# A second expert block on whole columns, its attention jobs inside the first block, and weight tiles scaled one step ahead

## The chip, the cores and the metric

The kernel runs on one core of a Trainium2 chip. The metric is the device time of one execution in microseconds (us); the time quoted for a version is the median of its timed runs. The profile is of one further execution.

## The reference

Three stages follow one another. First a recurrent attention (WKV) over 768 positions, for 4 batch entries and 8 heads of width 48; then two mixture layers over the 3072 tokens, the first of width 2048, the second, behind an RMS norm, gated and of width 1536. All inputs and the output are float32.

```python
def _attn_ref(r, k, v, w, u):
    for t in range(S):
        cur = np.einsum('bhd,bhe->bhde', u[None] * kt, vt)
        y[:, :, t] = np.einsum('bhd,bhde->bhe', rt, state + cur)
        state = wt[:, :, :, None] * state + np.einsum('bhd,bhe->bhde', kt, vt)

def _moe_ref(x, w_in, w_out):
    h = x @ w_in
    return (h * np.clip(h + 3.0, 0.0, 6.0) / 6.0) @ w_out

def _moe2_ref(x, w_gate, w_val, w_out, rms_g):
    xn = x / np.sqrt(np.mean(x * x, axis=-1, keepdims=True) + 1e-06) * rms_g
    g = xn @ w_gate
    return (g / (1.0 + np.exp(-g)) * (xn @ w_val)) @ w_out
```

## The kernel before, in words

The sequence is cut into 6 chunks of 128 positions. A chunk `c` of one batch entry `b` is a **job** (24 of them, job number 4c + b). The four jobs of a chunk give 512 token columns, and the first mixture layer takes these 512 columns as one **block**. Six blocks of the first layer come one after another, and behind them six of the second layer.

A block of the first layer is 16 tiles `f` of its width. Each is a **step**: `ff1` multiplies the tile's first weights with the 512 columns (all three parts of 128 rows), ScalarE and VectorE apply the activation (`emit_act`), and `ff2` multiplies the result with the tile's second weights into three accumulators. `ff2` of a step is put off by two steps (`todo`, L615), so that the activation has time. `LAGS` (L33) says for each block how many of its first tiles are done in two halves of 256 columns: first all of them on the left half, then all on the right half, then the remaining tiles on 512 columns. With `LAGS` (5, 8, 0, ...) block 0 has steps 0 to 20 (ten half steps, eleven whole ones), block 1 has steps 21 to 44 (sixteen half steps, eight whole ones), and block 2 begins at step 45.

Block 0 multiplies float32 weights directly (`emit_h_f32`, `emit_out_f32`). All other blocks use weights and activations that are split in two float32r parts and make three passes (`PASS`); the first part is a rounded copy, the second the rest.

The weights of the first layer arrive as 64-bit words. For each tile, `Weight.load` fetches the words into `raw` (L132), `scale` makes a scaled copy `mag` on ScalarE (L140), `bits` puts the float32 words together in three VectorE operations (L145 to L148) and has SyncE's queue copy them to their place `wpair` (L153), and `parts` splits them for the blocks behind block 0 (L159 on ScalarE, L160 on VectorE). `raw` has two buffers and `mag` one.

The order of all engines is that in which the program is written (`pin` fixes it). Lists named `before`, `between` and `behind` hold what is written ahead of a step's `ff1`, between its `ff1` and the put-off `ff2`, and behind that. `plan(j, n)` (L442) spreads job `j` over the steps from `n` on: the two scans of the decay (`scans`, L182) and GpSimd's `bonus1` (L209, L210) at step n; `muls` (L205), the reduction `bonus2` (L214) and GpSimd's `decay` at n+1; `fill` (eight ScalarE copies, L240), TensorE's `pe_a` (L259) and `pe_kt` (L247), and VectorE's masked copy `choose` (L265) at n+2; `pe_y` (L295, L301) and `pe_u` (L274) at n+3, with `copy_y` (L307) and eight small transfers `x<-y` (L310 to L313); and `split` (L323 on ScalarE, L324 on GpSimd), which writes the job's 128 columns of `xt`, the input of the block, at n+5. `pe_y` reads what `choose` wrote. The loads of job j+2 are written behind step n+3, the load of `rks` for job j+1 behind step n+1.

Jobs 0 to 3 are done in the prologue and in steps 0 to 6. Jobs 4 to 7, which feed block 1, start at steps 11, 15, 19 and 23 (L470), so jobs 6 and 7 end inside block 1: the right half of block 1 begins at step 29. Jobs of later chunks start at `first[c] - 18 + 4 * b`, that is 27, 31, 35 and 39 for the four that feed block 2. `begun` (L476) says at which step a weight tile is scaled and put together: `scale` is written ahead of that step's `ff1`, `bits` behind it, and then the load of the tile two further on. `parts` of tile f stands ahead of step f + 11. The norm of block 0's output (`Norm`) takes its operations at steps 24 to 36.

```python
    for f, n in begun.items():
        before[n] += [wa[f].scale]
        behind[n] += [wa[f].bits]
        if f + 2 < F1:
            behind[n] += [wa[f + 2].load]
    for f in range(F1):
        before[f + 11] += [wa[f].parts]
```

Of the kernel before, what the change touches and what calls it, by code (L numbers as in the profile page):

```python
# [9 lines left out]
F32 = mybir.dt.float32  # L10
F32R = mybir.dt.float32r
U32 = mybir.dt.uint32
U64 = mybir.dt.uint64
# [4 lines left out]
B, H, S, D = 4, 8, 768, 48  # L18
# [4 lines left out]
DM = H * D  # L23
KT = DM // 128
F1 = 2048 // 128
# [4 lines left out]
NB = 3 * F2 // 2  # L30
NX = 5
NE = 10
LAGS = (5, 8, 0, 0, 0, 0)  # L33


@with_exitstack
def kernel(
# [17 lines left out]
    def pool(stack, name, bufs=1, **kw):  # L55
        return stack.enter_context(tc.tile_pool(name=name, bufs=bufs, **kw))
# [9 lines left out]
    wp = pool(ctx, "wp", side="left")  # L66
    xt_p = pool(ctx, "xt", 2, side="left")
    rg_p = pool(ctx, "rg", 3, side="left")
    nm_p = pool(ctx, "nm", side="left")
    actx = ctx.enter_context(ExitStack())  # L70
    at_p = pool(actx, "at", 2, side="left")
    a1_p = pool(actx, "a1", side="left")
# [1 line left out]
    st_p = pool(tctx, "st", 2, side="left")  # L74
# [32 lines left out]
    def pin():  # L107
        fresh = []
        for x in reversed(nc.cur_bb.bb.instructions):
            if x.name in pinned:  # L110
                break
            fresh.append(x)
        for x in reversed(fresh):
            pinned.add(x.name)
            if x.engine in ENGINES:
                if x.engine in newest:
                    tc.add_manual_dep(x, newest[x.engine], NOSYNC, reason="program order")
                newest[x.engine] = x.name
# [2 lines left out]

    mag_bufs = 1

    class Weight:
        def __init__(self, src, dst, pairs):
            self.src, self.dst, self.pairs, self.near = src, dst, pairs, False

        def load(self):  # L130
            self.raw = st_p.tile([128, 2 * DM], U64, tag="raw", name="raw", bufs=2)
            nc.sync.dma_start(out=self.raw, in_=self.src.rearrange("p a n -> p (a n)"))  # L132

        def words(self):
# [1 line left out]
            return bits[:, :, 0], bits[:, :, 1]  # L136

        def scale(self):
            self.mag = st_p.tile([128, 2 * DM], F32, tag="mag", name="mag", bufs=mag_bufs)
            nc.scalar.activation(out=self.mag, in_=self.words()[1].bitcast(F32), func=AF.Copy, scale=2.0 ** -112)  # L140

        def bits(self):
# [230 lines left out]
    def emit_out(acc, slot, g, first, last, cols, parts=False):  # L373
        for m in range(KT):
            for j, (l, r) in enumerate(PASS):
                nc.tensor.matmul(  # L376
                    acc[m][:, cols], slot[:, l, m * 128:(m + 1) * 128], g[:, r, :],
                    start=(first and j == 0), stop=(parts or last and j == 2),
                    skip_group_check=parts and not (first and j == 0))
# [50 lines left out]
    jobs = [Job(c, b) for c in range(NC_) for b in range(B)]  # L430
    wa = [Weight(wa_d[f], None, False) for f in range(F1)]
    whole, halves = slice(0, TOK), (slice(0, HT), slice(HT, TOK))
    steps, first = [], []
    for c, lag in enumerate(LAGS):
        first.append(len(steps))
# [4 lines left out]
    before, between, behind = ([[] for _ in steps] for _ in range(3))  # L440

    def plan(j, n):  # L442

        jb = jobs[j]
        before[n] += [jb.scans, jb.bonus1]
        before[n + 1] += [jb.muls, jb.bonus2, jb.decay]
        before[n + 2] += [jb.fill]
        between[n + 2] += [jb.pe_a, jb.pe_kt, jb.choose, jb.copy_kt]
        between[n + 3] += [jb.pe_y, jb.pe_u, jb.copy_y, jb.add_u]
        if j + 2 < len(jobs):  # L450
            behind[n + 3] += [lambda: jobs[j + 2].load("w", "rk", "v")]
        if j + 1 < len(jobs):
            behind[n + 1] += [lambda: jobs[j + 1].load("rks")]
        before[n + 5] += [jb.split]


    j0, j1, j2, j3 = jobs[:B]
# [8 lines left out]
    for j, n in enumerate((1, 2, 3, 4)):  # L466
        behind[n] += [jobs[j].decay]
        between[n + 1] += [jobs[j].pe_kt, jobs[j].copy_kt]
        between[n + 2] += [jobs[j].pe_u, jobs[j].add_u]
    for j, n in zip(range(B, 2 * B), (11, 15, 19, 23)):  # L470
        plan(j, n)
    for c in range(2, NC_):
        for b in range(B):
# [1 line left out]

    begun = {f: f - 2 for f in range(2, W1)} | {7: 7, 8: 8} | {f: f + 1 for f in range(9, F1)}  # L476
    for f, n in begun.items():
        before[n] += [wa[f].scale]
        behind[n] += [wa[f].bits]
        if f + 2 < F1:  # L480
            behind[n] += [wa[f + 2].load]
    for f in range(F1):
        before[f + 11] += [wa[f].parts]
    behind[7] += [lambda: jobs[4].load("w", "rk", "rks", "v")]
    behind[9] += [lambda: jobs[5].load("w", "rk", "v")]

    def norm_plan(c, n, last):

# [10 lines left out]
    def ff1(c, f, cols):  # L499
        n = cols.stop - cols.start  # L500
        ps = ps_h.tile([128, n], F32, tag="h", name="hps")
        if c == 0:
            if cols.start:
                wa[f].x = wpair[f][:, :, 1, :].bitcast(F32)
            emit_h_f32(wa[f].x[:, 0], xts[c][:, :, :, cols], ps)
            g = rg_p.tile([128, n], F32, tag="g", name="g")
            emit_act(ps, n, g)
        else:
            emit_h(wpair[f][:, 0], xts[c][:, :, :, cols], ps)
            a = rg_p.tile([128, n], F32, tag="a", name="a", bufs=2)  # L510
            emit_act(ps, n, a)
            g = emit_split(a, n)
        x = wa[f].x[:, 1] if c == 0 else wpair[f][:, 1]
        todo.append(lambda: ff2(c, f, cols, g, x))

    def ff2(c, f, cols, g, x):
# [6 lines left out]
        else:  # L523
            emit_out(acc, x, g, first, last, cols, LAGS[c] > 0)
        if last:
            norms[c] = Norm(c, acc)

    def run(fs):
        for x in fs:
            x()  # L530

    def load_x(c):
        x = xt_p.tile([128, KT, 2, TOK], F32R, tag="xt", name="xt")
        raw = b_p.tile([128, KT, TOK], F32, tag="xraw", name="xraw", bufs=1)
        nc.sync.dma_start(out=raw, in_=xn_d[c])
        xns[c] = x

        def part(k):
            nc.scalar.activation(out=x[:, k, 0, :], in_=raw[:, k, :], func=AF.Copy)
            nc.vector.tensor_tensor(  # L540
                out=x[:, k, 1, :], in0=raw[:, k, :], in1=x[:, k, 0, :].bitcast(F32), op=ALU.subtract)
        return part
# [22 lines left out]
    nc.sync.dma_start(out=ub, in_=u_d.to_broadcast([128, DM]))  # L565
    nc.sync.dma_start(out=gain, in_=g_d)
    wa[2].load()
    wa[3].load()
    nc.vector.memset(dd, 0.0)
    nc.vector.memset(half, 0.5)  # L570
    nc.vector.memset(eps, 1e-6)
# [4 lines left out]
        wa[f].dst = wpair[f]  # L576
        wa[f].near = f < 2
    run((j0.scans, j0.pairs, j0.pe_bonus, j0.muls, j0.fill, j0.pe_a, j1.scans, j1.pairs, j1.pe_bonus, j1.muls))
    run((j0.choose, j1.fill, j1.pe_a, j0.pe_y0, wa[0].scale, wa[0].bits, j1.choose, j1.pe_y0))
    run((j0.copy_y0, wa[1].scale, wa[1].bits, j1.copy_y0, j2.scans))  # L580
    pin()


    for n, (c, f, cols) in enumerate(steps):
        if n == W1:
            sctx.close()
            wp2 = pool(ctx, "wp2", side="right", reuse_waits="tile")
            wpair += [wp2.tile([128, 2, 2, DM], F32R, name=f"wpair{i}") for i in range(W1, F1)]
            for i in range(W1, F1):
                wa[i].dst = wpair[i]  # L590
        if n == first[1]:
            tctx.close()
        if n == first[NC_ - 1]:
            actx.close()
            st_p = pool(ctx, "st2", 2, side="left", reuse_waits="tile")
            mag_bufs = 2
            b_p = pool(ctx, "bp", 2, side="left", reuse_waits="tile")
            bw_p = pool(ctx, "bw", side="left", reuse_waits="tile")
            begun2 = {f: f * NE // F1 for f in range(F1) if (f + 1) * NE // F1 > f * NE // F1}
            extra += [bw_p.tile([128, 2, 2, DM], F32R, name=f"bpair{i}") for i in range(NX)]  # L600
            wb = [Weight(wb_d[i], extra[i] if i < NX else wpair[i - NX], True) for i in range(NB)]
            wb[0].load()
            wb[1].load()
        run(before[n])
        if c == NC_ - 1:
            if f == 4:
                part = load_x(0)
            if 8 <= f < 8 + KT:
                part(f - 8)

            if f - 2 in begun2:
                wb[begun2[f - 2]].parts()
        ff1(c, f, cols)
        run(between[n])
        while len(todo) > 2:  # L615
            todo.pop(0)()
        if c == NC_ - 1 and f in begun2:
            wb[begun2[f]].scale()
        run(behind[n])
        if c == NC_ - 1 and f in begun2:  # L620
            wb[begun2[f]].bits()
            wb[begun2[f] + 2].load()
        pin()
# [145 lines left out]
```

## Time and profile before

| | |
|---|---|
| median of 3 runs | 1025.42 us (1025.32 to 1026.27) |
| the profiled execution: its own time | 1027.49 us |
| its span, first to last instruction | 1025.7 us |
| TensorE (PE) busy | 982.3 us, 96% of the span |
| TensorE weight load (PEld) | 782.4 us, 76% |
| VectorE (DVE) | 484.3 us, 47% |
| ScalarE (ACT) | 393.9 us, 38% |
| GpSimd (POOL) | 346.4 us, 34% |
| mean granted TensorE clock | 0.987 |

The busy share of an engine is a mean over stages that differ much, so the slices and the stretches by stage are read before it. PEclk is the granted clock as a share of full speed: 1.00 is 2.4 GHz, and a lower value is a mean of stretches at 2.4 and at 1.2 GHz. Matmuls are pipelined, so the time from one start to the next start says what one costs; the duration of a row is longer than that. A matmul of float32 operands shows as two records.

### The profile page before, as it was taken

To read this page: it belongs to the slowest core of one execution; us is meant where nothing else is said; L and a number is where in the kernel's file an instruction comes from. 1 tells how busy PE (TensorE), PEld (TensorE's weight loads), DVE (VectorE), ACT (ScalarE), POOL (GpSimd) and SP (SyncE) were. 2 spreads that over 40 slices of the span, in tenths; PEclk is the share of its full clock that TensorE was granted. 3 is DMA by queue.
4 is the path that set the end of the run, shared out by engine and by line. 5 is a ranking of instruction groups with operands and counts; after the bars stand their busy time and mean duration, and the time that the engine had idled before them with its cause. 6 is when DMAs were issued, how large, how long until landed. Compare 5 with 4: busy or idle time off the path is not lost.

```text
span 1025.7 us, 13752 instructions
## 1 busy us (share of the span) xinstructions
PE 982.3 (96%) x5385; PEld 782.4 (76%) x5385; DVE 484.3 (47%) x627; ACT 393.9 (38%) x753; POOL 346.4 (34%) x306
## 2 busy tenths in 40 slices
PE   5797998889999999999999999999999999999998
PEld 4674457877888888787787788888888888888886
DVE  7848756665457646665389996112112112112111
ACT  3433535544544454455356554222222222222212
POOL 0002214545465574565353352222222222222221
PEclk9899989999999999999999999999999999999999
DMA  8557522333322332231242450200100100100000
GB/s 320 173 202 276 183 90 81 123 130 102 122 76 79 120 134 75 109 92 64 100 144 103 156 182 1 93 1 1 62 1 1 61 1 1 62 1 1 31 1 31
DMA packets 36768, 91.92 MB, mean 90 GB/s; under 512 B 5984, under 2 KB 17120, under 8 KB 36704
## 3 DMA queue, kind: packets, MB, share of 16 engines
q1 hardware_dynamic: 36704, 91.05, 25.6%
q8 instruction: 42, 0.69, 0.3%
q14 instruction: 22, 0.18, 0.0%
HBM read 71.37 MB, written 9.44 MB: 79 GB/s over the span
## 4 chain that ended last, share of the span: by engine, by line
PE 79%; DVE 9%; ACT 4%; DMA 4%; issue 3%; SPq 1%; POOL 0%; ACTq 0%; DVEq 0%; POOLq 0%
PE o L376 27%; PE gps L347 14%; PE vps L347 14%; PE hps L347 12%; DMA raw<-in_dram 3%; PE aps L259 2%; PE yps L301 2%; DVE x L146 2%; PE o L359 2%; PE yps L295 1%; DVE x L148 1%; PE hps L353 1%; DVE a L365 1%; PE ktp L247 1%; DVE w L182 1%
## 5 line engine op out<-in xcount | busy, mean ns | idle before, releaser
L376 PE MATMUL o<-g,wpair 128*128 128x512 f32 (+1 forms) x1287 | 306.1, 382 | 0.0
L376 PEld LDWEIGHTS o<-g,wpair 128*128 128x128 f32 x1287 | 230.4, 189 | 48.8 <-issue 0.7
L370 POOL TENSOR_TENSOR g<-s,g 128x512 fp32r<-128x512 f32 x72 | 96.8, 1344 | 338.4 <-ACT g L369 338.4
L663 DVE TENSOR_TENSOR s<-s,vps 128x512 f32<-128x512 f32 x72 | 49.5, 687 | 301.3 <-PE vps L347 300.4
L347 PE MATMUL hps<-xt,wpair 128*128 128x512 f32 (+1 forms) x792 | 182.9, 375 | 3.4 <-POOL xt L324 2.1
L370 POOL TENSOR_TENSOR g<-a,g 128x512 fp32r<-128x512 f32 (+1 forms) x88 | 113.9, 1295 | 196.7 <-ACT g L369 185.4
L347 PEld LDWEIGHTS hps<-xt,wpair 128*128 128x128 f32 x792 | 139.7, 188 | 34.2 <-POOL xt L324 2.3
L347 PE MATMUL vps<-xt,wpair 128*128 128x512 f32 x486 | 120.4, 392 | 0.0
L365 DVE SCALAR_TENSOR_TENSOR a<-a,hps 128x512 f32<-128x512 f32 (+1 forms) x88 | 55.7, 633 | 129.3 <-ACT a L364 129.2
L347 PE MATMUL gps<-xt,wpair 128*128 128x512 f32 x432 | 107.2, 392 | 0.0
L369 ACT ACTIVATE g<-s 128x512 fp32r<-128x512 f32 x72 | 45.5, 632 | 159.7 <-DVE s L663 159.7
L347 PEld LDWEIGHTS vps<-xt,wpair 128*128 128x128 f32 x486 | 91.2, 188 | 20.5
L660 ACT ACTIVATE s<-gps 128x512 f32<-128x512 f32 x72 | 43.0, 597 | 158.7 <-PE gps L347 158.7
L347 PEld LDWEIGHTS gps<-xt,wpair 128*128 128x128 f32 x432 | 81.0, 188 | 18.3
L364 ACT ACTIVATE a<-hps,half 128x512 f32<-128x512 f32 (+1 forms) x88 | 56.6, 643 | 96.1 <-PE hps L347 89.5
L369 ACT ACTIVATE g<-a 128x512 fp32r<-128x512 f32 (+1 forms) x88 | 52.2, 593 | 87.8 <-DVE a L365 86.2
L182 DVE TENSOR_TENSOR_SCAN w<-w,dd 128x520 f32<-128x520 f32 x48 | 74.8, 1559 | 4.6 <-DMA w<-in_dram 2.9
L240 ACT ACTIVATE a<-iperm,cb 128x128 f32<-128x128 f32 x192 | 58.5, 387 | 0.1
L347 PE MATMUL gps<-xt,bpair 128*128 128x512 f32 x216 | 53.0, 390 | 0.0
L209 POOL TENSOR_TENSOR rks<-rks 128x384 f32<-128x384 f32 x20 | 29.2, 1460 | 64.7 <-DMA rks<-in_dram 64.7
L347 PEld LDWEIGHTS gps<-xt,bpair 128*128 128x128 f32 x216 | 40.5, 188 | 8.8
L140 ACT ACTIVATE mag<-raw 128x768 f32<-128x768 f32 x34 | 30.6, 901 | 41.1 <-DMA raw<-in_dram 30.3
(85 smaller groups left out, 1055.8 us busy)
## 6 DMA issues: line engine op xcount, KB each, us to landing
raw<-in_dram SPq DMA_DIRECT2D x34, 768.0 KB, 4.7
w<-in_dram SPq DMA_DIRECT2D x24, 520.0 KB, 3.8
rk<-in_dram SPq DMA_DIRECT2D x24, 512.0 KB, 4.6
rks<-in_dram SPq DMA_DIRECT2D x20, 384.0 KB, 4.7
v<-in_dram SPq DMA_DIRECT2D x24, 256.0 KB, 4.8
wpair<-x SPq DMA_DIRECT2D x16, 384.0 KB, 3.2
xn<-x SPq DMA_DIRECT2D x6, 768.0 KB, 4.0
xraw<-xn SPq DMA_DIRECT2D x6, 768.0 KB, 5.0
```

Of the source, the lines that this page charges most:

```text
L140: nc.scalar.activation(out=self.mag, in_=self.words()[1].bitcast(F32), func=AF.Copy, scale=2.0 ** -112)
L182: nc.vector.tensor_tensor_scan(out=x, data0=x, data1=dd.rearrange("p a h j -> p (a h j)"), initial=0.0, op0=ALU.mult, op1=ALU.add)
L209: nc.gpsimd.tensor_tensor(out=x, in0=x, in1=self.rks[:, 1, :], op=ALU.mult)
L240: nc.scalar.activation(out=self.head(h), in_=iperm, func=AF.Copy, scale=self.cb[:, h, :])
L347: nc.tensor.matmul(ps, slot[:, l, k * 128:(k + 1) * 128], xt[:, k, r, :], start=(k == 0 and j == 0), stop=(k == KT - 1 and j == 2))
L364: nc.scalar.activation(out=a, in_=ps, func=AF.Relu, scale=1.0 / 6.0, bias=half)
L365: nc.vector.scalar_tensor_tensor(out=a, in0=a, scalar=1.0, in1=ps, op0=ALU.min, op1=ALU.mult)
L369: nc.scalar.activation(out=g[:, 0, :], in_=a, func=AF.Copy)
L370: nc.gpsimd.tensor_tensor(out=g[:, 1, :], in0=a, in1=g[:, 0, :].bitcast(F32), op=ALU.subtract)
L376: nc.tensor.matmul(acc[m][:, cols], slot[:, l, m * 128:(m + 1) * 128], g[:, r, :], start=(first and j == 0), stop=(parts or last and j == ...
L660: nc.scalar.activation(out=s, in_=gp, func=AF.Silu)
L663: nc.vector.tensor_tensor(out=s, in0=s, in1=vp, op=ALU.mult)
```

## The change

Block 1 is done on whole columns (`LAGS` (5, 0, ...)): it has 16 whole steps, 21 to 36, and block 2 begins at step 37. Jobs 4 to 7 start at steps 6, 9, 12 and 15, three steps apart, and end at step 20, inside block 0. The first loads of jobs 4 and 5 stand behind steps 2 and 4. `parts` of tile f stands ahead of step f + 17, so 12 of 16 tiles are split inside block 1. The buffers of `raw` are three and of `mag` two; `scale` stands at the end of the step ahead of that of `bits`, and the load is for the tile three further on. The pool of the norm's tiles is opened on the other side of the memory when block 1 begins.

```diff
-LAGS = (5, 8, 0, 0, 0, 0)
+LAGS = (5, 0, 0, 0, 0, 0)
...
-            self.raw = st_p.tile([128, 2 * DM], U64, tag="raw", name="raw", bufs=2)
+            self.raw = st_p.tile([128, 2 * DM], U64, tag="raw", name="raw", bufs=2 if self.pairs else 3)
...
-            self.mag = st_p.tile([128, 2 * DM], F32, tag="mag", name="mag", bufs=mag_bufs)
+            self.mag = st_p.tile([128, 2 * DM], F32, tag="mag", name="mag", bufs=2)
...
-    for j, n in zip(range(B, 2 * B), (11, 15, 19, 23)):
+    for j, n in zip(range(B, 2 * B), (6, 9, 12, 15)):
         plan(j, n)
...
-        before[n] += [wa[f].scale]
+        (behind[n - 1] if n else before[n]).append(wa[f].scale)
         behind[n] += [wa[f].bits]
-        if f + 2 < F1:
-            behind[n] += [wa[f + 2].load]
+        if f + 3 < F1:
+            behind[n] += [wa[f + 3].load]
     for f in range(F1):
-        before[f + 11] += [wa[f].parts]
-    behind[7] += [lambda: jobs[4].load("w", "rk", "rks", "v")]
-    behind[9] += [lambda: jobs[5].load("w", "rk", "v")]
+        before[f + 17] += [wa[f].parts]
+    behind[2] += [lambda: jobs[4].load("w", "rk", "rks", "v")]
+    behind[4] += [lambda: jobs[5].load("w", "rk", "v")]
...
-    wa[3].load()
...
-    run((j0.choose, j1.fill, j1.pe_a, j0.pe_y0, wa[0].scale, wa[0].bits, j1.choose, j1.pe_y0))
-    run((j0.copy_y0, wa[1].scale, wa[1].bits, j1.copy_y0, j2.scans))
+    run((j0.choose, j1.fill, j1.pe_a, j0.pe_y0, wa[0].scale, wa[0].bits, wa[3].load, j1.choose, j1.pe_y0))
+    run((j0.copy_y0, wa[1].scale, wa[1].bits, wa[4].load, j1.copy_y0, j2.scans))
...
         if n == first[1]:
             tctx.close()
+            nm_p = pool(ctx, "nm", side="right", reuse_waits="tile")
```

Three places show how the order moves. The changed file has three or four lines fewer at its head, so L140 of before is L137 of the change.

On ScalarE, at the job whose `fill` comes first behind a weight tile. Before, steps 12 and 13, with job 4's `fill`:

```order
L140 ACTIVATE mag<-raw 128x768
L159 ACTIVATE wpair_116<-wpair_116 128x2x384
L364 ACTIVATE g<-hps,half 128x512
L240 ACTIVATE a<-iperm,cb 128x128 x8
L140 ACTIVATE mag<-raw 128x768
L159 ACTIVATE wpair_117<-wpair_117 128x2x384
L364 ACTIVATE g<-hps,half 128x512
L252 ACTIVATE kt<-ktp 128x512
```

The change, end of step 10 and step 11, with job 5's `fill` and, ahead of it, the `split` of job 4:

```order
L137 ACTIVATE mag<-raw 128x768
L320 ACTIVATE xt<-x 128x3x128
L237 ACTIVATE a<-iperm,cb 128x128 x8
L361 ACTIVATE g<-hps,half 128x512
L249 ACTIVATE kt<-ktp 128x512
L137 ACTIVATE mag<-raw 128x768
```

The scaled copy and the split weights no longer stand between `fill` and the activation `g<-hps`; the `split` of the job before now stands ahead of `fill`.

On VectorE, from a job's `muls` to its `choose`. Before, job 5, steps 16 and 17:

```order
L205 TENSOR_TENSOR rk<-rk,w 128x8x64 x2
L214 TENSOR_REDUCE cb<-rks 128x8
L160 TENSOR_TENSOR wpair_120<-wpair_120 128x2x384
L365 SCALAR_TENSOR_TENSOR g<-g,hps 128x512
L145 TENSOR_SCALAR x<-raw 128x768
L146 SCALAR_TENSOR_TENSOR x<-raw,x 128x768
L148 SCALAR_TENSOR_TENSOR x<-mag,x 128x768
L160 TENSOR_TENSOR wpair_121<-wpair_121 128x2x384
L365 SCALAR_TENSOR_TENSOR g<-g,hps 128x512
L265 COPY_PREDICATED a<-mask,aps 128x512 x2
```

The change, job 6, steps 13 and 14:

```order
L202 TENSOR_TENSOR rk<-rk,w 128x8x64 x2
L211 TENSOR_REDUCE cb<-rks 128x8
L362 SCALAR_TENSOR_TENSOR g<-g,hps 128x512
L142 TENSOR_SCALAR x<-raw 128x768
L143 SCALAR_TENSOR_TENSOR x<-raw,x 128x768
L145 SCALAR_TENSOR_TENSOR x<-mag,x 128x768
L362 SCALAR_TENSOR_TENSOR g<-g,hps 128x512
L262 COPY_PREDICATED a<-mask,aps 128x512 x2
```

The two weight splits between `muls` and `choose` are gone from block 0.

On TensorE, from the first `ff1` of block 1 on. Before, steps 21 to 23, with job 6 (`st_108`):

```order
L347 MATMUL hps<-xt,wpair_115 128x256 x9
L259 MATMUL aps<-rk 128x128 x8
L247 MATMUL ktp<-ident,rk 128x128 x4
L359 MATMUL o_432<-g,wpair_598 128x512
...
L347 MATMUL hps<-xt,wpair_116 128x256 x9
L295 MATMUL yps<-rk,st_108 64x128 x8
L301 MATMUL yps<-a,v 64x128 x8
L274 MATMUL ups<-v,kt 64x48 x8
```

The change, with job 8 (`st_103`):

```order
L344 MATMUL hps<-xt,wpair_112 128x512 x9
L256 MATMUL aps<-rk 128x128 x8
L244 MATMUL ktp<-ident,rk 128x128 x4
L356 MATMUL o_431<-g,wpair_619 128x512
...
L344 MATMUL hps<-xt,wpair_113 128x512 x9
L292 MATMUL yps<-rk,st_103 64x128 x8
L298 MATMUL yps<-a,v 64x128 x8
L271 MATMUL ups<-v,kt 64x48 x8
```

The matmuls between a job's `pe_a` and its `pe_y` have 512 columns in place of 256, and the job at that place feeds block 2, not block 1.

## Rows read from the trace of the kernel before

**Rows 1.** The page, busy tenths of TensorE in 40 slices of 25.6 us.

```profile
PE   5797998889999999999999999999999999999998
```

**Rows 2.** Stretches: length, then busy us per engine, granted clock, DMA share, GB/s.

```profile
61.10:147.40 86.30, 77.77 (x333) 43.37 (x332) 58.65 (x79) 32.97 (x62) 16.01 (x17) 0.94 0.55 195
147.40:258.10 110.70, 98.65 (x838) 84.61 (x837) 65.10 (x98) 54.84 (x124) 56.13 (x62) 0.95 0.32 107
258.10:341.00 82.90, 82.90 (x564) 66.73 (x563) 49.38 (x64) 39.54 (x84) 47.60 (x42) 1.00 0.28 94
```

**Rows 3.** TensorE's waits from 24 to 259 us: total us, times, longest.

```profile
PE yps L295 <- DVE a L265: 8.5, 3, 3.4
PE yps L295 <- POOL g L370: 6.7, 2, 4.4
PE ktp L247 <- ACT st L281: 3.0, 3, 1.4
...
PE hps L347 <- POOL xt L324: 2.1, 1, 2.1
```

**Rows 4.** Timeline of TensorE behind job 4's `pe_y`: start us, us, operation.

```profile
102.87 3.95 PE L359 MATMUL o<-g,wpair 128*128 128x512 f32 x6
```

**Rows 5.** ScalarE's longest kind of wait from 61.1 to 147.4 us: total us, times, longest.

```profile
ACT mag L140 <- DMA raw<-in_dram: 27.5, 6, 8.3
```

**Rows 6.** Timeline of TensorE across the end of block 0.

```profile
140.10 2.74 PE L359 MATMUL o<-g,wpair 128*128 128x512 f32 x6
142.67 2.74 PE L353 MATMUL hps<-xt,wpair 128*128 128x512 f32 x6
...
148.98 1.16 PE L259 MATMUL aps<-rk 48*128 48x128 f32 x16
...
150.56 2.74 PE L359 MATMUL o<-g,wpair 128*128 128x512 f32 x6
...
154.30 0.67 PE L295 MATMUL yps<-rk,st 64*64 64x128 f32 x16
...
156.37 1.98 PE L359 MATMUL o<-g,wpair 128*128 128x512 f32 x4
```

**Rows 7.** Groups by form: count, busy us, mean ns, idle before.

```profile
L182 DVE TENSOR_TENSOR_SCAN w<-w,dd 128x520 f32<-128x520 f32 x48 | 74.8, 1559 | 4.6 <-DMA w<-in_dram 2.9
...
L205 DVE TENSOR_TENSOR rk<-rk,w 128x512 f32<-128x512 f32 x48 | 43.6, 947 | 0.1
...
L160 DVE TENSOR_TENSOR wpair<-wpair 128x768 fp32r<-128x768 f32 x16 | 15.8, 989 | 18.3 <-ACT wpair L159 18.3
...
L159 ACT ACTIVATE wpair<-wpair 128x768 fp32r<-128x768 f32 x16 | 13.3, 831 | 0.0
...
L364 ACT ACTIVATE g<-hps,half 128x512 f32<-128x512 f32 x11 | 7.4, 677 | 9.1 <-PE hps L353 9.1
```

**Rows 8.** Timeline of ScalarE in steps 3 and 4; in brackets the idle time before, and what ended it.

```profile
48.05 0.90 ACT L140 ACTIVATE mag<-raw 128x768 f32<-128x768 f32 x1 [3.06 <-DVE x L148]
...
53.45 0.89 ACT L140 ACTIVATE mag<-raw 128x768 f32<-128x768 f32 x1 [1.83 <-DMA raw<-in_dram]
```

**Rows 9.** Timeline of ScalarE at job 4: `fill`, `copy_y`, `split`.

```profile
91.29 2.43 ACT L240 ACTIVATE a<-iperm,cb 128x128 f32<-128x128 f32 x8
...
104.76 0.59 ACT L307 ACTIVATE y<-yps 128x512 f32<-128x512 f32 x1
...
111.81 0.52 ACT L323 ACTIVATE xt<-x 128x384 fp32r<-128x384 f32 x1 [0.70 <-DMA x<-y]
```

**Rows 10.** Timelines of VectorE and GpSimd during job 4's scans.

```profile
79.66 1.89 DVE L182 TENSOR_TENSOR_SCAN w<-w,dd 128x520 f32<-128x520 f32 x1
...
80.54 1.81 POOL L210 TENSOR_TENSOR rks<-rks,ub 128x384 f32<-128x384 f32 x1
```

**Rows 11.** Timelines of VectorE and TensorE at job 13, in block 2.

```profile
282.94 1.37 DVE L265 COPY_PREDICATED a<-mask,aps 128x512 f32<-128x512 uint32 x2
...
286.48 0.67 PE L295 MATMUL yps<-rk,st 64*64 64x128 f32 x16
```

More of the change, by code (lines that the diff above doesn't have):

```diff
@@ L68 @@
     rg_p = pool(ctx, "rg", 3, side="left")
-    nm_p = pool(ctx, "nm", side="left")
     actx = ctx.enter_context(ExitStack())
@@ L118, in pin @@
                 newest[x.engine] = x.name
-    mag_bufs = 1
     class Weight:
@@ L595 @@
             st_p = pool(ctx, "st2", 2, side="left", reuse_waits="tile")
-            mag_bufs = 2
             b_p = pool(ctx, "bp", 2, side="left", reuse_waits="tile")
```

## The prediction

> **What bounds the kernel now.** I read the slices first, then the stretches by stage, then the waits of TensorE, and last what stands ahead of the late instruction on its own engine. In the slices [rows 1] TensorE is busy nine tenths or more from the tenth slice to the last but one; the lower digits lie in the first quarter, and that is where this change works. The stretches [rows 2] put it in time: from the first matmul of step 6 (61.1 us) to that of step 21 (147.4) TensorE is busy 77.8 of 86.3 us at a granted clock of 0.94, in block 1 (to 258.1) 98.6 of 110.7 at 0.95, while block 2, which has the same 16 tiles and four jobs, takes 82.9 us, is busy all of it and stays at 1.00. The two first stretches thus lose 8.5 and 12.1 us to idle time, and more to the clock's lower level.
>
> TensorE's own waits [rows 3] name `pe_y` first: 8.5 us for `choose`, and 6.7 us put down to GpSimd, and then the inputs `xt` of block 1's right half. After such a wait the clock is low: six records that take 2.74 us at full speed [rows 6] take 3.95 behind job 4's `pe_y` [rows 4]. The masked copy is late because VectorE and ScalarE are late, and ScalarE is late because the scaled copy `mag` stands ahead of its other work and waits for its weight tile: 27.5 us in six waits, the longest 8.3 [rows 5]. In block 1's half steps the cause is another: between a job's `pe_a` and `pe_y` TensorE has only two passes of 256 columns, half of what block 2 has there, so that `fill` and `choose` can't keep up.
>
> **The change part by part.**
>
> *Block 0, step 6 to step 21.* TensorE's work, if nothing waits: a float32 pass of 512 columns costs 142.67 - 140.10 = 2.57 us, a half one is taken at half of it, 1.29; a job's `pe_a` and `pe_kt` cost 150.56 - 148.98 = 1.58 and its `pe_y` and `pe_u` 156.37 - 154.30 = 2.07, together 3.65 [rows 6]. In these steps stand 20 whole and 10 half passes (ff1 of steps 6 to 20, ff2 of steps 4 to 18) and now four jobs: 51.4 + 12.9 + 14.6 = 78.9 us, where 86.3 were [rows 2]: -7.4, though two more jobs are done in it.
>
> *Block 1.* It has become block 2's shape: 82.9 us [rows 2], of which 68.3 without the four jobs is 2.13 a pass. Two of its first ff2 passes are float32 ones, + 2 x (2.57 - 2.13) = 0.9. So 83.8 in place of 110.7: -26.9. Whole in place of half columns is in this number; it is a small part of it.
>
> Both together take 162.7 us for 197.0. The 34.3 us between them are 20.6 of idle time and 13.7 of busy time (176.4 - 162.7), nearly all of which is work at the lower clock. So this counts on both: no idle time, and a clock that therefore stays up.
>
> *Scaling a step ahead.* Ahead of step 6 three waits of `pe_kt` for ScalarE sum to 3.0 us [rows 3]. In two of them a scaled copy stood in front, waiting 3.06 us for VectorE to free the one `mag`, and 1.83 us for the tile [rows 8]; the second buffer of `mag`, the third of `raw` and the earlier load remove both. The third wait is the job's own chain. Bounds 0 and 3.0; I take 1.5, since a chain of that kind remains at all three places. In block 0 the same edit removes the 27.5 us [rows 5], which cover the -7.4 above and are not counted again.
>
> *VectorE as cover.* It is busy 58.7 us of the 86.3 [rows 2]. Block 0 gains two full jobs: two scans, two `muls` (1.56 and 0.95 each, means over the run [rows 7]), a masked copy of 1.37 [rows 11] and an allowance of 1.0 for two small operations, 7.4 each; it loses six splits of 0.99 [rows 7]. 58.7 + 14.8 - 5.9 = 67.6 under 78.9: still covered, with less to spare. The earlier loads of jobs 4 and 5 cost nothing on the same ground: transfers have a share of 0.55 in this stretch [rows 2].
>
> *New waits.* (a) `split` of job 4 now stands ahead of job 5's `fill` on ScalarE and waits for eight `x<-y` transfers. From `copy_y` to `split` 111.81 - 104.76 = 7.05 us passed [rows 9]; with `split` 0.52, `fill` 2.43 [rows 9], the activation 0.68 [rows 7] and as much again on VectorE, `choose` 1.37 [rows 11], it ends 12.7 us behind the first `pe_y`. Until then TensorE has job 4's `pe_u` (about 0.5), three half passes of 1.29, three whole ones of 2.57 and job 5's `pe_a` and `pe_kt` of 1.58 to do: 13.7. So 1.0 us is left. If it fails, `pe_y` of job 5 waits and the two activations behind it, not yet due, don't. Behind `copy_y` SyncE's queue also holds job 6's loads and the next tile, which have two steps. (b) The split weights now stand ahead of `choose` in block 1: 0.83 on ScalarE and 0.99 on VectorE [rows 7], against 286.48 - 284.31 = 2.2 us by which block 2's `choose` is early [rows 11]. Each of (a) and (b) is bounded by 0 and the old wait of 3.4 [rows 3]; both come out near the edge of their cover, so I take 1.0 for each.
>
> *The pool for the norm* moves to other memory; no engine gets an instruction for it, and its tiles are first written in step 22, long behind the old tenants: 0. From block 2 on nothing changes, and TensorE has no gap there to be filled.
>
> **Sum.** -7.4 - 26.9 - 1.5 + 2.0 = -33.8 us. The profiled execution took 1027.49 us, which makes 993.7; it stands 2.1 above the median of the runs, so the median should go from 1025.4 to **991.6**.
>
> **Rivals.**
>
> *Block 0's jobs keep their waits* (0.13). Three steps are less room than four, and half steps less again. Each job would lose 3.4 of wait [rows 3] and 1.2 of clock (3.95 - 2.74 [rows 4, 6]), 4.6 each: with two of four 9.2, so 1001; with all four 18.4, so 1010. For it: `choose` was 3.4 late with five us of TensorE work to hide in. Against it: the waits for tiles and the splits that made it late are gone from there.
>
> *VectorE is held by GpSimd and becomes block 0's bound* (0.08). Job 4's first scan took 1.89 us while GpSimd's `bonus1` ran [rows 10], against a mean of 1.56 [rows 7]. GpSimd is busy 16.0 us in this stretch [rows 2] with two and a half jobs, so about 26 with four. If all of that stood in VectorE's way on top of its 67.6, 93.6 would exceed 78.9 by 14.7 and the time be 1006. The Trainium skill (SBUF, "Who interferes with whom") says that a VectorE instruction with two SBUF inputs and a GpSimd one that reads SBUF exclude each other for the whole instruction. In the rows the scan is longer by less than the operation beside it (1.81 [rows 10]), and it decides only where VectorE has no room, so I hold it less likely than cover.
>
> *The splits make block 1's jobs late* (0.07). Three jobs (8, 9, 10) have them; at 3.4 each 10.2, so 1002.
>
> *Slower than before* (0.03). SyncE's queue is in order. A job's loads wait there for tiles that TensorE and GpSimd still read; the next weight tile stands behind them. If tiles then come later than the two steps of lead, the scaled copy holds ScalarE at each of the four jobs as it did, by up to 8.3 [rows 5], with 1.2 of clock: 4 x 9.5 = 38, more than the 35.8 gained, so 1028. It needs all four at their worst.
>
> *The change does not do what it says* (0.02): no gain, 1025. The order of the engines speaks against it: the scaled copies and splits do stand elsewhere.
>
> **Chances and range.** The forecast has 0.67 and reaches from 987 (new waits 0, the startup's 3.0 whole, and about a us less than counted) to 997 (both new waits at their bound). Up to 1003 the range takes in the splits' case and the smaller half of the first rival. A difference of 0.2%, some 2 us, is what the measurement can tell from none: faster is the forecast and the three rivals behind it, 0.95; of the 0.02 without effect 0.015 is same and 0.005 falls to slower, with the 0.03 of the queue: 0.035.
>
> **What would show it.** Right: step 6 begins 1 to 2 us earlier; block 0 from there takes about 80 us and block 1 about 84, both at a granted clock of 0.98 or more; ScalarE's wait of the scaled copy for tiles is below 5 us in block 0; `pe_y` has no wait above 1 us. Wrong: `pe_y` still waits for `choose` in steps 9 to 18 with VectorE busy (first two rivals) or idle (ScalarE late); block 1 shows three waits of `pe_y`; or the wait for `raw` is back.

## The result and the profile after

The changed kernel takes 993.49 us (median of 4 runs, 992.94 to 994.07), the kernel before, on the same chip, 1025.85 (4 runs): a ratio of 0.9682 with a 95% interval of 0.9665 to 0.9699. The profiled execution took 993.44 us with a span of 991.5, where before took 1027.49 with 1025.7. In two of the experiments below (halves, and halves with more room) the profiled execution was slow, 1954 and 3402 us: the ratios leave it out, the medians hold it and are raised by under 0.4 us, and the traces are those of a second run.

The page's slices of TensorE, which answer to [rows 1]: from the third to the last but one all are at nine tenths or more.

```profile
PE   5899999999999999999999999999999999999998
```

The two stretches, with the columns of [rows 2], from step 6's first matmul to block 1's and from there to block 2's:

```profile
59.12:139.76 80.64, 80.64 (x469) 46.66 (x468) 65.49 (x91) 37.39 (x78) 25.06 (x28) 1.00 0.68 237
139.76:224.28 84.52, 84.21 (x559) 65.71 (x557) 60.23 (x76) 47.59 (x91) 47.74 (x40) 1.00 0.24 84
```

| stretch | before, us | after, us | difference | forecast |
|---|---|---|---|---|
| start to step 6 | 61.1 | 59.1 | -2.0 | -1.5 |
| step 6 to block 1 | 86.3 | 80.6 | -5.7 | -7.4 |
| block 1 | 110.7 | 84.5 | -26.2 | -26.9 |
| block 2 to the end | 767.6 | 767.2 | -0.4 | 0 |

The +2.0 us of the forecast for new waits stand in none of these rows.

TensorE is busy all of the first stretch and all but 0.3 us of the second, at a granted clock of 1.00, where it was 0.94 and 0.95. Its waits from 24 to 240 us, beside [rows 3]: the 8.5 and 6.7 us of `pe_y` have shrunk to 0.3, and the three waits of `pe_kt` from 3.0 to 1.5.

```profile
PE ktp L244 <- ACT st L278: 1.5, 3, 0.5
...
PE yps L292 <- DVE a L262: 0.3, 1, 0.3
```

ScalarE's waits from 59.1 to 139.8 us: the wait of the scaled copy for its tile, 27.5 us in [rows 5], is 8.8, and the longest kind is now that of the activation for TensorE, which is how it looks when TensorE is the bound.

```profile
ACT g L361 <- PE hps L350: 25.3, 11, 4.4
ACT mag L137 <- DMA raw<-in_dram: 8.8, 3, 4.8
```

### The profile page after: what moved, and what is told of

Read it like the earlier page. It is cut to its first block, busy times and chain, and to the rows that moved or that the text cites. A ratio compares the mean times of both kernels' runs of the same rounds, so it can differ in the third digit from the quotient of the medians.

```text
span 991.5 us, 13431 instructions
## 1 busy us (share of the span) xinstructions
PE 971.0 (98%) x5241; PEld 767.0 (77%) x5241; DVE 489.6 (49%) x619; ACT 391.7 (40%) x737; POOL 351.2 (35%) x298
## 3 DMA queue, kind: packets, MB, share of 16 engines
q1 hardware_dynamic: 36704, 91.05, 26.2%
## 4 chain that ended last, share of the span: by engine, by line
PE 87%; DVE 7%; ACT 3%; issue 2%; DMA 1%; SPq 0%; DVEq 0%; ACTq 0%
PE o L373 28%; PE gps L344 15%; PE vps L344 15%; PE hps L344 12%; PE hps L350 4%; PE o L356 4%; PE aps L256 2%; PE yps L298 2%; DVE a L362 1%; PE yps L292 1%; DVE w L179 1%; PE ktp L244 1%; DVE x L143 1%; PE ups L271 1%; DVE wpair L157 1%
## 5 line engine op out<-in xcount | busy, mean ns | idle before, releaser
L373 PE MATMUL o<-g,wpair 128*128 128x512 f32 (+1 forms) x1215 | 303.0, 394 | 0.0
L373 PEld LDWEIGHTS o<-g,wpair 128*128 128x128 f32 x1215 | 224.5, 188 | 51.2 <-issue 0.7
L344 PE MATMUL hps<-xt,wpair 128*128 128x512 f32 x720 | 180.6, 395 | 0.2 <-DVE a L362 0.2
L367 POOL TENSOR_TENSOR g<-a,g 128x512 fp32r<-128x512 f32 x80 | 113.5, 1419 | 182.7 <-ACT g L366 174.3
L344 PEld LDWEIGHTS hps<-xt,wpair 128*128 128x128 f32 x720 | 134.8, 188 | 33.4 <-DVE a L362 1.4
L362 DVE SCALAR_TENSOR_TENSOR a<-a,hps 128x512 f32<-128x512 f32 x80 | 54.5, 681 | 108.5 <-ACT a L361 108.5
L361 ACT ACTIVATE a<-hps,half 128x512 f32<-128x512 f32 x80 | 54.5, 682 | 89.6 <-PE hps L344 83.8
L366 ACT ACTIVATE g<-a 128x512 fp32r<-128x512 f32 x80 | 50.6, 632 | 88.7 <-DVE a L362 87.2
L202 DVE TENSOR_TENSOR rk<-rk,w 128x512 f32<-128x512 f32 x48 | 45.6, 989 | 0.1
```

Source lines behind the costliest of these rows:

```text
L202: nc.vector.tensor_tensor(out=x, in0=x, in1=s[:, :, :, 0:HF], op=ALU.mult)
L344: nc.tensor.matmul(ps, slot[:, l, k * 128:(k + 1) * 128], xt[:, k, r, :], start=(k == 0 and j == 0), stop=(k == KT - 1 and j == 2))
L361: nc.scalar.activation(out=a, in_=ps, func=AF.Relu, scale=1.0 / 6.0, bias=half)
L362: nc.vector.scalar_tensor_tensor(out=a, in0=a, scalar=1.0, in1=ps, op0=ALU.min, op1=ALU.mult)
L366: nc.scalar.activation(out=g[:, 0, :], in_=a, func=AF.Copy)
L367: nc.gpsimd.tensor_tensor(out=g[:, 1, :], in0=a, in1=g[:, 0, :].bitcast(F32), op=ALU.subtract)
```

## The experiments

All differ from the kernel before or after by one part of the change, or by a small addition. They ran on several chips, on which the kernel before took 1024.4 to 1026.2 us, so the ratios to it are what is compared.

| kernel | median, us | ratio to before, 95% | step 6 begins | block 0 from there | block 1 |
|---|---|---|---|---|---|
| before | 1025.85 | | 61.1 | 86.3 | 110.7 |
| jobs early only | 1018.78 | 0.9945 (0.9925 to 0.9966) | 58.8 | 91.5 | 98.5 |
| weight path only | 1012.42 | 0.9871 (0.9850 to 0.9893) | 60.1 | 74.2 | 112.3 |
| change with halves | 1013.26 | 0.9876 (0.9859 to 0.9892) | 60.2 | 80.6 | 103.3 |
| halves, splits early | 1009.23 | 0.9848 (0.9826 to 0.9869) | 59.3 | 82.3 | 98.2 |
| halves, more room | 1010.09 | 0.9842 (0.9824 to 0.9860) | 59.5 | 83.0 | 98.6 |
| change, old weight path | 1004.25 | 0.9787 (0.9773 to 0.9802) | 61.5 | 91.1 | 84.5 |
| change, splits early | 995.83 | 0.9707 (0.9692 to 0.9721) | 59.2 | 82.9 | 84.1 |
| change, copy not ahead | 995.33 | 0.9711 (0.9690 to 0.9731) | 60.3 | 81.6 | 84.5 |
| start reordered | 995.68 | 0.9692 (0.9672 to 0.9712) | 61.2 | 80.6 | 84.5 |
| one `choose` earlier | 994.92 | 0.9707 (0.9688 to 0.9727) | 60.6 | 80.7 | 84.5 |
| the change | 993.49 | 0.9682 (0.9665 to 0.9699) | 59.1 | 80.6 | 84.5 |

The start of step 6 says less than the other columns: the first matmul of all begins at 7.8 to 9.8 us, a spread that no edit explains.

### Half columns kept in block 1

```diff
-LAGS = (5, 0, 0, 0, 0, 0)
+LAGS = (5, 8, 0, 0, 0, 0)
```

> The changed kernel with block 1's first eight tiles in two halves again (jobs 4 to 7 still inside block 0, splits still deferred, scaling still ahead). Theory (the gain of block 1 is idle time and low clock behind pe_y, because half steps leave too little room between a job's pe_a and its pe_y): jobs 8 to 10 fall into the half steps and wait again, some 1 to 4.5 us each, with low clock behind the longer waits, and the half form itself costs about 1 us: 1000 to 1008, with the lost time in block 1 and pe_y waits of 5 to 11 us there. Rival 1 (the width of the matmuls itself brought block 1's 26 us): 1015 or more, without long waits. Rival 2 (only having the jobs 4 to 7 early counts): 994 to 996.

Measured: 1013.26 us, between the theory and the first rival, so neither holds as it was put. The kernel ran again for its trace (1012.65, 2 runs):

> The version with block 1's first eight tiles in halves once more, for its trace. Its time was 1013, more than the 1000 to 1008 of the theory's waits and less than the 1015 of the width. Theory, widened: in the half steps the deferred splits make VectorE and ScalarE the bound: a half step gives TensorE 2.1 us and a quarter job 0.9, VectorE 0.41 + 0.99 + 1.85 = 3.25. Then jobs 8 and 9, and the passes behind them, wait for VectorE or ScalarE by 3 to 5 us each between steps 21 and 33, and not later. Width: block 1 is long without waits above 1 us.

Block 1 with the columns of [rows 2], and behind it the longest four of TensorE's waits there (7 rows, 12.6 us in all).

```profile
140.90:244.20 103.30, 90.85 (x702) 77.70 (x701) 63.55 (x91) 51.56 (x111) 53.50 (x55) 0.95 0.24 82
```

The waits, with the columns of [rows 3]:

```profile
PE yps L292 <- POOL g L367: 4.8, 2, 3.0
PE hps L344 <- DVE a L362: 2.1, 1, 2.1
PE yps L292 <- DVE a L262: 1.8, 1, 1.8
PE aps L256 <- ACT wpair L156: 1.5, 1, 1.5
```

`pe_y` is late (the first row and the third), but `ff1` also waits for VectorE's activation and `pe_a` for ScalarE, which was at a split of weights. The waits at jobs 8 and 9 come, but the longest is 3.0 us where 3 to 5 each were expected. So it isn't the one distance that the forecast named.

### Halves with the splits as early as before

In addition to the edit above:

```diff
-        before[f + 17] += [wa[f].parts]
+        before[f + 11] += [wa[f].parts]
```

> The changed kernel with block 1's first eight tiles in halves and the splits at f + 11 (so that only five or six are left in block 1). Theory: half steps without the splits give back only the waits that jobs 9 and 10 had in the kernel before (2.4 and 1.8 us, with some low clock behind) and about 1 us for the form: 1000 to 1006. Rival (the width of the matmuls itself): as slow as with the splits deferred, 1010 or more.

Measured: 1009.23, longer than the theory's range and just short of the rival's bound. Block 1 takes 98.2 us, 5.1 less than with the splits inside it, so deferred splits do cost where steps are short. Still TensorE waits 7.5 us, its clock is 0.95, and its work alone is 90.76 us where whole columns need 84.21.

```profile
141.56:239.79 98.23, 90.76 (x703) 77.79 (x701) 56.88 (x85) 47.49 (x105) 50.20 (x55) 0.95 0.25 86
```

### Halves with one more step between `pe_a` and `pe_y`

In addition, `pe_y`, `pe_u`, `copy_y`, the loads behind them and `split` of jobs 8 to 10 stand a step later:

```diff
+        d = int(j in (8, 9, 10))
-        between[n + 3] += [jb.pe_y, jb.pe_u, jb.copy_y, jb.add_u]
+        between[n + 3 + d] += [jb.pe_y, jb.pe_u, jb.copy_y, jb.add_u]
...
-        before[n + 5] += [jb.split]
+        before[n + 5 + d] += [jb.split]
```

> The version with halves and early splits (1009.2), with pe_y, pe_u, the copy, the next loads and the split of jobs 8, 9 and 10 one step later, so that about two half passes more stand between choose and pe_y. Theory (the halves cost time because they leave too little room between pe_a and pe_y): the waits of pe_y, 4.3 us in block 1, go, and the low clock behind them; what stays are the waits of the first passes for VectorE, about 3 us, and 1 us for the form: 1001 to 1005. Rival (the cost lies in the half form or in the many short instructions, wherever pe_y stands): 1008 to 1010, block 1 still 97 us or more.

Measured: 1010.09, no gain on the 1009.23 without it (ratios of 0.9842 and 0.9848), as the rival had it. So the room between `pe_a` and `pe_y` alone, on which the forecast's reading of block 1 stood, falls as the cause. The kernel ran again for its trace (1009.77, 2 runs):

> The version with halves, early splits and pe_y of jobs 8 to 10 one step later, for its trace. It took 1010.1, no less than the 1009.2 without the extra room, so the room between pe_a and pe_y alone is not what the halves cost. Theory, changed: in half steps all distances that are counted in steps are half as long in time (two buffers of ff1's accumulator, ff2 two steps behind, a job's parts one step apart), so each burst of other work on VectorE, ScalarE or GpSimd stops TensorE somewhere; with pe_y later, its waits go and waits of ff1 for the activation, of pe_a and of ff2 for the split take their place: idle time in block 1 6 to 9 us as before, in other rows. Rival: the waits are gone and the time sits in work at the low clock or in the form: idle below 4 us, block 1 still 97 or more.

The first three of TensorE's four waits in block 1:

```profile
PE hps L344 <- DVE a L362: 5.2, 3, 2.6
PE aps L256 <- issue: 1.6, 2, 1.4
PE hps L344 <- DVE dd L184: 1.2, 1, 1.2
```

The wait of `pe_y`, 4.3 us without the extra room, is gone. In its place `ff1` waits 5.2 us for VectorE's activation, where it waited 0.2, and TensorE's waits sum to 8.4 us where they were 7.5: the theory as changed. A half pass takes half the time of a whole one, so every distance that is counted in steps is half as long in time, and when one was widened the next became the bound.

The run without the extra room shows what half columns cost block 1 of the change with early splits, 98.2 - 84.1 = 14.1 us. Waits make 7.5 of it. The granted clock of 0.95 over 98.2 us makes about 4.9 at most (an estimate: 0.05 of the stretch). The half form makes one to two: a half pass costs 1.08 us, where half of a whole one is 1.02 to 1.05, 32 times. So the shorter matmuls by themselves are the small part; the waits that come with short steps, and the low clock with them, are the large one. Two half passes of that run, and behind them two whole ones of the change:

```profile
151.41 1.24 PE L344 MATMUL hps<-xt,wpair 128*128 128x256 f32 x9
152.49 1.24 PE L373 MATMUL o<-g,wpair 128*128 128x256 f32 x9
...
157.52 2.20 PE L344 MATMUL hps<-xt,wpair 128*128 128x512 f32 x9
159.56 2.20 PE L373 MATMUL o<-g,wpair 128*128 128x512 f32 x9
```

### The change with the old weight path

`raw` with two buffers, `mag` with one, the scaled copy in the step of its `bits`, loads for the tile two further on, as in the kernel before:

```diff
-        (behind[n - 1] if n else before[n]).append(wa[f].scale)
+        before[n] += [wa[f].scale]
...
-        if f + 3 < F1:
-            behind[n] += [wa[f + 3].load]
+        if f + 2 < F1:
+            behind[n] += [wa[f + 2].load]
```

> The changed kernel with the old weight path (raw two buffers, mag one, scaled ahead of its own step's ff1, load two tiles on); jobs early, whole columns and deferred splits stay. Theory (in block 0 the scaled copy's wait for its tile holds ScalarE, and with it fill, activation and choose): step 6 begins about 2 us later, the wait of the scaled copy for tiles is 15 us or more in block 0, and the four jobs wait up to 3.4 us each with low clock behind: 1002 to 1014. Rival (it was the splits that made choose late, and scaling ahead only brings the start's 2 us): 995 to 997.

Measured: 1004.25, in the theory's range, though not by its sizes: two jobs wait, one of them 6.9 us where up to 3.4 was expected, and the copy's wait for tiles is 13.2 us where 15 or more was. The waits of `pe_y` in block 0 come back, the longest at job 6, and ahead of them on ScalarE those of the scaled copy. Waits of both engines from 61.4 to 152.5 us:

```profile
PE yps L294 <- DVE a L264: 7.6, 2, 6.9
...
ACT mag L139 <- DMA raw<-in_dram: 13.2, 2, 7.9
ACT mag L139 <- DVE x L147: 8.3, 2, 4.2
...
ACT mag L139 <- DVE dd L186: 4.0, 1, 4.0
```

Block 0 takes 91.1 us at a clock of 0.94; block 1 is as after. This is the first rival of the forecast, brought about by taking the cover away.

### The weight path alone

The kernel before with three buffers of `raw`, two of `mag`, the copy a step ahead, the load three tiles ahead, and the norm's pool moved to make room (the reverse of the diff above, in before).

> The kernel before with the new weight path alone (raw three buffers, mag two, scaled a step ahead, load three tiles on, the norm's tiles on the other side); jobs, halves and splits as before. Theory: step 6 begins 2 us earlier, jobs 4 and 5 no longer wait 3.4 us each in block 0 and the clock stays up there, so block 0 is 6 to 9 us shorter; block 1 keeps its waits of about 12 us: 1014 to 1019. Rival (scaling ahead only brings the start's 2 us): 1023 to 1025.

Measured: 1012.42, better than both cases. Block 0 loses 12.1 us, where 6 to 9 were expected, though TensorE's idle time in it fell by 7.3 only (8.5 to 1.3): the clock came up too, from 0.94 to 1.00. Block 1 keeps its waits (6.9 us of `pe_y` put down to GpSimd, 2.2 of `xt`). The two stretches, with the columns of [rows 2] (this execution took 1016.07, the longest of its four):

```profile
60.10:134.26 74.16, 72.89 (x333) 40.68 (x332) 58.80 (x79) 33.58 (x62) 17.84 (x17) 1.00 0.61 215
134.26:246.56 112.30, 101.39 (x838) 87.14 (x837) 65.64 (x98) 54.92 (x124) 56.21 (x62) 0.92 0.31 106
```

### The jobs early alone

```diff
-    for j, n in zip(range(B, 2 * B), (11, 15, 19, 23)):
+    for j, n in zip(range(B, 2 * B), (6, 9, 12, 15)):
...
-    behind[7] += [lambda: jobs[4].load("w", "rk", "rks", "v")]
-    behind[9] += [lambda: jobs[5].load("w", "rk", "v")]
+    behind[2] += [lambda: jobs[4].load("w", "rk", "rks", "v")]
+    behind[4] += [lambda: jobs[5].load("w", "rk", "v")]
```

> The kernel before with jobs 4 to 7 at steps 6, 9, 12, 15 and their loads early, nothing else. Theory (block 0 has no room for four jobs while the scaled copy waits for its tile and ten splits stand in it; what jobs 6 and 7 no longer lose in block 1 comes back in block 0): block 0 95 to 104 us, block 1 86 to 92, 1015 to 1025. Rival (having the jobs early is the gain): 1005 or less.

Measured: 1018.78, in the theory's range, but divided otherwise: both blocks miss theirs, block 0 by being shorter (91.5) and block 1 by being longer (98.5). Block 0 grows by 5.2 us and block 1 shrinks by 12.2, to the length that it has with half columns in the run with early splits. TensorE waits 8.5 us for `choose` in block 0, and ScalarE's scaled copy 24.7 in the three rows shown; the waits of both from 58 to 151 us:

```profile
PE yps L295 <- DVE a L265: 8.5, 2, 6.7
...
ACT mag L140 <- DVE dd L187: 10.2, 2, 5.6
ACT mag L140 <- DVE x L148: 9.1, 2, 4.5
ACT mag L140 <- DMA raw<-in_dram: 5.4, 1, 5.4
```

### The change with the splits early

The edit of `parts` alone (f + 11) in the changed kernel.

> The changed kernel with the weight splits back at f + 11, so ten of them in block 0 instead of four. Theory (VectorE has room for six more splits of 0.99 us, and only job 5's choose, which ends 0.2 us ahead of its need, is late by a split on ScalarE and VectorE): 994 to 997.5, block 0 longer by 1 to 3 us, block 1 shorter by 0 to 0.5. Rival (the splits were what made choose late): each of the jobs 5 to 7 waits 2 us or more, 1001 or more.

Measured: 995.83, as the theory had it. Six more splits go into block 0, VectorE is busy 72.8 us of it, and `pe_y` waits twice (jobs 5 and 6, where job 5 alone was expected). Block 0, with the columns of [rows 2]:

```profile
59.25:142.18 82.93, 80.87 (x470) 46.83 (x468) 72.78 (x98) 41.32 (x84) 27.41 (x28) 1.00 0.66 231
```

TensorE's only wait in it:

```profile
PE yps L292 <- DVE a L262: 2.0, 2, 1.4
```

### The change with the copy not ahead

Buffers and loads as in the change, only `scale` back in the step of its `bits`.

> The changed kernel with the scaled copy back ahead of its own step's ff1, but with the third raw and second mag buffer and the load three tiles on. Theory (the copy's wait came from the tile's late load; with the load a step earlier the place of the copy matters little): 993 to 996. Rival (the place of the copy is what frees ScalarE): 998 or more, with the copy's wait for tiles again above 12 us in block 0.

Measured: 995.33; the interval overlaps that of the change. In the trace block 0 is 0.9 us longer, with one wait of `pe_y` of 0.8: the theory holds. So most of the weight path's gain is the buffers and the earlier loads; the copy's place adds about one us.

### The start reordered

Two attempts to win what is left ahead of step 6. In the first, VectorE does job 2's `scans` and `muls` ahead of the second tile's `bits`, and its `choose` ahead of job 3's `scans`; in the second only the last of these.

```diff
-    before[0] += [j2.pairs, j2.muls]
...
-    before[1] += [j3.scans, j2.choose]
+    before[1] += [j2.choose, j3.scans]
...
-    run((j0.copy_y0, wa[1].scale, wa[1].bits, wa[4].load, j1.copy_y0, j2.scans))
+    run((j0.copy_y0, wa[1].scale, j2.scans, j2.pairs, j2.muls, wa[1].bits, wa[4].load, j1.copy_y0))
```

> The changed kernel with VectorE's order changed in the start alone: job 2's scans, pairs and muls ahead of the second weight tile, and job 2's choose ahead of job 3's scans. The waits there in the changed kernel are 2.1 us for pairs and 1.3 us for choose, with low clock behind. Theory (TensorE waits for VectorE's order): step 6 begins 1 to 3 us earlier, 990.5 to 992.5. Rival (VectorE is the bound of the whole start, so that its order only moves the waits): 993 to 994, step 6 at 59 us.

> The changed kernel with job 2's choose ahead of job 3's scans, the one half of the start's reordering that touches no weight tile. Theory (VectorE is the bound of the start; what TensorE does not wait for choose it waits for job 3's pairs and muls, and the clock's level in the start decides the rest): no gain beyond 1 us, 992.5 to 994.5. Rival (the 1.3 us wait is TensorE's own and comes back whole): 992 or less.

Measured: 995.68 and 994.92, above the theories' ranges by 3.2 and 0.4: no gain. The five executions of the first attempt fall in two groups: two took 992.3 and 992.5 us at a mean granted clock of 0.997, three 995.7 to 996.3 at 0.992 to 0.993. The trace is of one of the three, so where the other two differ isn't shown. Two stretches of it, with the columns of [rows 2]:

```profile
24.00:36.00 12.00, 7.97 (x69) 6.25 (x68) 11.61 (x19) 5.94 (x15) 0.19 (x1) 0.88 0.72 269
36.00:48.00 12.00, 11.92 (x55) 9.45 (x57) 7.80 (x11) 5.03 (x14) 0.00 (x0) 0.55 0.30 105
```

The same of the change:

```profile
24.00:36.00 12.00, 8.57 (x46) 6.23 (x47) 11.69 (x20) 5.16 (x13) 0.38 (x2) 0.67 0.76 279
36.00:48.00 12.00, 11.71 (x122) 9.91 (x116) 9.08 (x15) 6.84 (x17) 0.00 (x0) 0.90 0.31 108
```

With the new order TensorE is busy 11.92 of the 12 us from 36 on but at a clock of 0.55, nearly all of it at the lower level; in the change it is 0.90, and the lower level lies ahead of that (0.67 against 0.88 from 24 to 36). Over both stretches together the clock is 0.72 against 0.79. `ff1` of step 2 begins 3 us earlier (35.6 against 38.6), and step 6 two us later.

## Why the prediction was right

The forecast of a gain by two mechanisms (no idle time, and so no stretch at the lower clock level) held: the profiled execution took 993.44 us where the sum made 993.7. The median is 1.9 above the forecast of 991.6, for the most part because I took the profiled execution of before to stand 2.1 above its median and carried that over; that of after stands on its median. That the sum came so near the profiled time is in part luck: blocks 0 and 1 came out 1.7 and 0.7 us longer than counted, and the 2.0 set aside for new waits, of which 0.3 came (within block 1's length), made up for most of that.

**Block 0 (-7.4 forecast, -5.7 measured).** There is no idle time left, and the clock is 1.00; the term was short of work. The stretch holds a fifth `pe_u`, that of job 3 in step 6, which the sum left out (0.6 us). And a pass next to a job's matmuls takes about 0.1 us more than one between two other passes, 14 times (1.4 us), while the last pass ahead of block 1 takes 0.4 less (2.17): 2.58 from the first to the second of these rows of TensorE's timeline, 2.66 from the second to the third.

```profile
93.64 2.74 PE L356 MATMUL o<-g,wpair 128*128 128x512 f32 x6
96.22 2.74 PE L350 MATMUL hps<-xt,wpair 128*128 128x512 f32 x6
98.88 1.16 PE L256 MATMUL aps<-rk 48*128 48x128 f32 x16
```

78.9 + 0.6 + 1.4 - 0.4 = 80.5, where 80.64 was measured. So of the 13.7 us of busy time the forecast put too much down to the lower clock: the granted clocks of before, 0.94 over 86.3 us and 0.95 over 110.7, allow about 10.7. The cover was counted well: VectorE is busy 65.5 us (67.6 forecast), GpSimd 25.1 (26).

**Block 1 (-26.9, measured -26.2).** The length was right, the reason in part wrong. The step that failed is "Whole in place of half columns is in this number; it is a small part of it", and ahead of it the reading that half steps are late because of the two passes between `pe_a` and `pe_y`. The runs make a path from before to after, one part at a time:

| part added | block 0 | block 1 | ratio to before |
|---|---|---|---|
| jobs early | +5.2 | -12.2 | 0.9945 |
| weight path | -9.2 | -0.3 | 0.9848 |
| whole columns | +0.6 | -14.1 | 0.9707 |
| splits deferred | -2.3 | +0.4 | 0.9682 |

In this order of adding them the whole columns are the largest part, 14.1 of block 1's 26.2 us, and widening the named room alone gained nothing. What they take away is mostly waits (7.5 us) at several places, and low clock (about 4.9 at most), and only one to two us of form. Each part also opens what the one before left: the jobs bring waits into block 0 that the weight path removes.

**The start (-1.5, measured -2.0).** The three waits of `pe_kt` went from 3.0 to 1.5 us, each to the same 0.5 of the job's own chain, as forecast. The other 0.5 lies within the spread of the first matmul (9.27 before, 8.92 after).

**New waits (+2.0, measured 0.3).** (a) The order of job 5 is tight but holds: `split` of job 4 ends, `fill` and the activation follow, and `choose` ends at 86.13, 0.2 us ahead of `pe_y`, where 1.0 was worked out. From `copy_y` to `split` 8.2 us passed, where 7.05 was taken from [rows 9]; that is the difference. Timelines of ScalarE, VectorE and TensorE:

```profile
72.53 0.60 ACT L304 ACTIVATE y<-yps 128x512 f32<-128x512 f32 x1 [1.19 <-PE yps L298]
...
80.72 0.52 ACT L320 ACTIVATE xt<-x 128x384 fp32r<-128x384 f32 x1 [2.22 <-DMA x<-y]
81.15 2.43 ACT L237 ACTIVATE a<-iperm,cb 128x128 f32<-128x128 f32 x8
...
84.79 1.34 DVE L262 COPY_PREDICATED a<-mask,aps 128x512 f32<-128x512 uint32 x2
...
86.31 0.67 PE L292 MATMUL yps<-rk,st 64*64 64x128 f32 x16
```

(b) In block 1 one of the three jobs with splits (job 10) waits, 0.31 us, behind a `choose` that a split and an activation had put off. The run with early splits shows the other side of this edge: 2.3 us more in block 0.

**What would show it.** Step 6 earlier, both stretches' lengths and clocks and no `pe_y` above 1 us: as forecast. ScalarE's wait for tiles below 5 us: no, 8.8. It did no harm, as the copy now stands a step ahead of what needs it.

**Rivals.** Waits kept in block 0: seen at such a size only with the old weight path (+10.8 us by the medians, where 9.2 to 18.4 had been worked out). SyncE's queue: no sign, since tiles are waited for less than before. VectorE held by GpSimd: it happens, but costs only some 0.9 to 1.7 us a job, by the records of block 0 against the same operations at their shortest. Timelines of VectorE and GpSimd at job 6's scans, beside [rows 10], and the first scan of job 7, when GpSimd was idle:

```profile
88.61 1.89 DVE L179 TENSOR_TENSOR_SCAN w<-w,dd 128x520 f32<-128x520 f32 x1
...
90.78 1.62 DVE L179 TENSOR_TENSOR_SCAN w<-w,dd 128x520 f32<-128x520 f32 x1
...
104.96 1.24 DVE L179 TENSOR_TENSOR_SCAN w<-w,dd 128x520 f32<-128x520 f32 x1
...
87.83 1.58 POOL L206 TENSOR_TENSOR rks<-rks 128x384 f32<-128x384 f32 x1 [5.51 <-DMA rks<-in_dram]
89.48 1.82 POOL L207 TENSOR_TENSOR rks<-rks,ub 128x384 f32<-128x384 f32 x1
```

The first scan ends 1.1 us behind GpSimd's first operation, about a scan's length alone (1.24); the second GpSimd operation ends 0.8 behind the scan, and the second scan 1.1 behind that. So they run in turn, and each record holds its wait for the other. The Trainium skill (SBUF — State Buffer, "Who interferes with whom") has it that a VectorE instruction with two SBUF inputs contends with a GpSimd one that reads SBUF, and calls the shared port pair an exclusive lock. The rows agree. The forecast's argument against it, that a scan grew by less than the operation beside it, was no argument: only the rest of that operation is waited for. What kept it from counting is that VectorE has 15 us to spare in block 0.

## What to carry to other kernels

Distances in a hand-written order that are counted in steps shrink with the step: before widening one of them, ask whether the step itself can be longer, and expect the next distance to become the bound if not. Where TensorE waits a few us at a time, read the granted clock of the stretch with the waits: 7.3 us of them gave 12.1 back. When a stage has no idle time left, count its work from pitches at the places where shapes change, and count what hangs over from the stage before.

## What was not expected of the hardware

One order of the program gave two granted clocks: with the start reordered, two of five executions had a mean of 0.997 and took 992.3 and 992.5 us, three had 0.992 to 0.993 and took about 3.5 us longer. In the traced one of the three an earlier start of TensorE's work lost what it gained, as 12 us of nearly unbroken matmuls ran at 0.55. What decides between the two stays open, and so does whether the new order by itself would gain a us.

GpSimd stretched VectorE to more than twice where several of its operations follow one another: in the run of halves with early splits a job's two `muls` took 2.79 us, where they take 1.29 with GpSimd idle. Timelines of VectorE and GpSimd there:

```profile
164.46 2.79 DVE L202 TENSOR_TENSOR rk<-rk,w 128x512 f32<-128x512 f32 x2
...
163.09 2.21 POOL L397 TENSOR_TENSOR sq<-sq 128x512 f32<-128x512 f32 x1
...
165.26 1.44 POOL L206 TENSOR_TENSOR rks<-rks 128x384 f32<-128x384 f32 x1
```
